# Feed-forward units of 128-token blocks: one slice of the inner width each, or two

## The chip, the core and the metric

The kernel runs on one core of a Trainium2 chip. Its time is the device time of one execution in microseconds (us), the median of three runs. The engines are named as in the profile: PE is TensorE (matmuls; PEld its weight loads), DVE is VectorE, ACT is ScalarE, POOL is GpSimd and SP is SyncE, which issues most DMAs.

## What is computed

Three stages follow each other: attention that keeps the 32 best scores of each row (4 batches, 8 heads, 576 tokens, head size 64), a feed-forward layer on the 2304 tokens that come out, and a layer of 8 experts of which each token uses one or none.

```
scores = (q @ k.T) / sqrt(64); keep those >= the 32nd largest of the row; softmax; x = attn @ v
h = x @ w_in                    # 2304 x 512 by 512 x 2048
r = max(h, 0); g = r * r
x = g @ w_out                   # 2304 x 2048 by 2048 x 512
out = x; tokens with x @ w_skip > 0: out = x + gate * (max(x @ w1[e], 0) @ w2[e]), e = argmax(x @ w_gate)
```

The change is in the second stage.

## The kernel before, in words

**Attention.** The main loop makes 76 ticks `j`. A tick takes one pair of score tiles (128 queries by 576 keys each). For the next pair `qk` (line 311) puts the scores into PSUM on PE and `evac_s` (line 330) copies them out on ACT (line 332); both have high priority. On DVE a tick is `tree` (line 355, work on line 360) for the next pair, `top32` (line 366: MAX8 and MATCH_REPLACE8 four times) and `mask` (line 404). ACT does the exponential (line 401) and its 16-bit high part (line 430), POOL multiplies by the mask (line 415) and takes the low part (line 435). Three ticks later `av` (line 445) multiplies by v on PE, `xout` scales the rows, and `x_split` (line 487) splits a finished block of 128 tokens into two 16-bit parts and sends it through a transposing DMA to `xt`.

**Groups and units.** Tokens come in groups (`group`, line 95): 14 groups of 128 tokens (the halved blocks, and the two `c` groups of the batches' first tokens) and 2 groups of 256. `add_units` (line 523) cuts a group that is ready, two ticks after its x was sent, into 16 units, one for each slice of 128 columns of the inner width 2048. A unit goes through four steps:

- `mm1` (line 529) on PE: 12 matmuls (line 535) of the group's tokens against one slice of `w_in`, as high x high, low x high and high x low parts, into a PSUM tile `ph` (two buffers of 256 columns).
- `act1` (line 540) on ACT: the copy through the rectifier `r` (line 543), the square `g` in 32 bits (line 545) and the square `gh` in 16 bits (line 547). `r` and `g` have two buffers, `gh` four; all are 256 columns wide, and a unit of 128 tokens uses half.
- `g_low` (line 553) on POOL: the remainder `g - gh` (line 556).
- `mm2` (line 561) on PE: for each 128 tokens three matmuls of 512 columns (line 568), accumulated in `px` over the 16 slices. Behind the last slice `finish` copies the rows out and stores them; transposes and logits for the experts' gate follow.

**The order.** `step_units(n)` (line 615) adds n to a credit and, while it holds one, takes the next unit: `mm1` of it, `act1` of the one before, `mm2` of the oldest whose remainder was asked for; it then takes off the unit's columns divided by 128. A tick calls it twice with 2.2 (`HALVES` is 4.4, line 40) and calls `g_low` once, later. Behind the attention the loop on line 913 drains what is left with `step_units(1, 1)`, `g_low` and the logits, one unit a turn. When the tokens of a stretch of groups are through, `route` (line 776) and `first_ids` (line 824) work out their experts on DVE, with small matmuls on PE (lines 797, 798, 801 and 831) and tiles `oh`, `cum` and `hit`; their entries are scattered to a table by POOL (line 837), one a turn and only while fewer than `DRAIN` = 12 units (line 52) are left. Ahead of this loop 16 chunks of the experts' weights are split on ACT, DVE and POOL (`next_chunk`, line 889). After it the last route, the scatters left over and the first gather (line 961) start the experts.

The queue of each engine is fixed when the program is built: the instructions are taken in the order of the source, high priority first, against a modelled timeline (line 1407), and an engine then runs its queue in that order.

Of the kernel before, what the change touches and what calls it, by code (L numbers as in the profile page):

```python
# [9 lines left out]
F32 = mybir.dt.float32  # L10
# [12 lines left out]
NTOK, DM, DFF = B * S, 512, 2048  # L23
# [25 lines left out]
ON_POOL = (4, 6)  # L49
BG = (3, 3, 2)  # L50
PRE = 16
DRAIN = 12
X_EXP, M_EXP = 12, 7
XBUFS = [4, 2, 2]
BUFS = {"qm": 2, "ql": 2, "qc": 2, "k": 4, "v": 8}
# [44 lines left out]
def attention_two_moes(ctx, tc, qm, qc, kd, vd, w_in, w_out, w_g, w1, w2, cst, out):  # L100
    nc = tc.nc
    const = ctx.enter_context(tc.tile_pool(name="const", bufs=1))
    dram = ctx.enter_context(tc.tile_pool(name="dram", bufs=1, space=DRAM))
    psum = ctx.enter_context(tc.tile_pool(name="psum", bufs=1, space=PSUM))
# [24 lines left out]
    wil = wpool.tile([128, 4, DFF], F16, name="wil")  # L129
    wol = wpool.tile([128, 16, DM], F16, name="wol")  # L130
    wih = wpool.tile([128, 4, DFF], F16, name="wih")
    woh = wpool.tile([128, 16, DM], F16, name="woh")
# [388 lines left out]
    units = []  # L521

    def add_units():
        while ready and tick[0] >= max(ready[0][1] + X_LAG, UNIT_START):
            gr = ready.pop(0)[0]
            for f in range(16):
                units.append(dict(gr=gr, f=f, n=128 * len(gr[1])))

    def mm1(u):
        x = xt[u["gr"]]  # L530
        ph = psum.tile([128, 256], F32, name="ph", bufs=2)[:, :u["n"]]
        n = 0
        for wt, c0 in ((wih, 0), (wih, 4), (wil, 0)):
            for d in range(4):
                nc.tensor.matmul(ph, lhsT=wt[:, d, u["f"] * 128:(u["f"] + 1) * 128], rhs=x[:, :, c0 + d, :],  # L535
                                 start=(n == 0), stop=(n == 11))
                n += 1
        u["ph"] = ph

    def act1(u):  # L540
# [18 lines left out]
    x2p = {}  # L559

    def mm2(u):
        f, gh, gr = u["f"], u["gh"], u["gr"]
        if f == 0:
            x2p[gr] = [psum.tile([128, DM], F32, name="px", bufs=2) for _ in gr[1]]
        for t, px in enumerate(x2p[gr]):
            n = 0
            for part, w in ((0, woh), (0, wol), (1, woh)):
                nc.tensor.matmul(px, lhsT=gh[:, part, t * 128:(t + 1) * 128], rhs=w[:, f, :],  # L568
                                 start=(f == 0 and n == 0), stop=(f == 15 and n == 2))
                n += 1  # L570
        if f == 15:
            finish(gr)

# [2 lines left out]
    def finish(gr):  # L576
        kk = gr[0]
        for px, t in zip(x2p[gr], gr[1]):
            n = column(kk, t)
            x2 = mpool.tile([128, DM], F32, name="x2", tag="x2", bufs=2)  # L580
            nc.scalar.activation(x2, px, AF.Copy, scale=2.0 ** -OUT_EXP)
            if kk == "c":
                for a in range(2):
                    r0 = (2 * t + a) * S
                    stores.append(nc.sync.dma_start(out[r0:r0 + 64, :], x2[64 * a:64 * a + 64, :]))
            else:
                r0 = kk[0] * S + 64 + 256 * kk[1] + 128 * t
                stores.append(nc.sync.dma_start(out[r0:r0 + 128, :], x2))
            logit_jobs.append((x2, n))
# [25 lines left out]
    def step_units(n, depth=0):  # L615
        add_units()
        credit[0] += n
        while credit[0] > 0.99:
            u = units.pop(0) if units else None
            if u:  # L620
                mm1(u)
            if started:
                act1(started.pop(0))
            if u:
                started.append(u)
            if len(lowered) > (depth if u else 0):
                mm2(lowered.pop(0))
            credit[0] -= u["n"] / 128 if u else 2
            if not u:
                credit[0] = min(credit[0], 0)  # L630
# [26 lines left out]
    start = by_j.pop(-1)  # L657
# [186 lines left out]
    wt = {}  # L844
# [63 lines left out]

    tick[0] = NJ + 9
    add_units()  # L910
    edge, marks = 0, [NT - 4, NT - 2] + [NT - 1] * (LAST in HALVED)
    pending = []
    while units or started or squared or lowered:
# [5 lines left out]
        while marks and min(left, default=NT) >= marks[0]:  # L919
# [3 lines left out]
            edge = marks.pop(0)  # L923
        if pending and len(units) < DRAIN:
            with tc.issue_after(g_last[0]):
# [485 lines left out]
```

## Time and profile before

| | us |
|---|---|
| median of 3 runs | 1027.3 |
| the three runs | 1027.3, 1023.33, 1030.25 |
| the profiled execution | 1023.65 |
| its span, first to last instruction | 1021.8 |

The profile is of one execution. Start times count from the beginning of the span; busy times are sums over one engine. A row of the timeline gives the start, the duration, the engine, the line, the operation, what it writes and reads, and in brackets how long its engine stood idle before it and what ended that. Operations of one kind in a row are merged (x2), and their durations overlap at the ends.

### The profile page before, as it was taken

Reading aid. Unit: us, or ns where it says so; the run is one execution under the profiler, and the core shown is the slowest. Engines: PE = TensorE matmul, PEld = TensorE weight load, DVE = VectorE, ACT = ScalarE, POOL = GpSimd, SP = SyncE. Lnnn points to the kernel's source line nnn. Section 1 sums busy time; section 2 is a strip of 40 time slices with the busy share of each in tenths; the row PEclk is TensorE's granted clock in tenths of the full one; section 3 lists DMA queues with packets and bytes.
Section 4 is the critical chain, followed back from the end, with each engine's and each line's share of the span. In section 5 each row is a group of like instructions: output and inputs, shape, how many; then the busy total and the mean of one; then the engine's idle time right before and its main releaser. Section 6 shows DMA issues by size and latency. Waiting matters only on the chain. (4 is left out here: it accounts for less than half of the span.)

```text
span 1021.8 us, 25759 instructions
## 1 busy us (share of the span) xinstructions
PE 779.8 (76%) x9036; PEld 592.5 (58%) x9036; DVE 845.7 (83%) x2279; ACT 759.8 (74%) x2117; POOL 767.4 (75%) x783
## 2 busy tenths in 40 slices
PE   0123337989879979989969999999997958688852
PEld 0122226767667757667657777767775746565631
DVE  4999999999999999999989999999908634535631
ACT  7777676899988998888779989999866642544620
POOL 4576777899879898888879988899955875744850
PEclk9999999999999999999979999999998978898876
DMA  9675554668675475565475676565537508653500
GB/s 286 174 189 152 141 126 78 103 137 156 118 161 111 94 150 94 108 130 119 100 137 121 138 138 130 116 117 90 96 64 269 208 27 326 214 177 113 177 15 10
DMA packets 257023, 138.16 MB, mean 135 GB/s; under 512 B 215348, under 2 KB 238260, under 8 KB 256848
## 3 DMA queue, kind: packets, MB, share of 16 engines
q1 hardware_dynamic: 253568, 132.16, 55.7%
q0 software_dynamic: 3280, 3.80, 1.2%
q8 instruction: 94, 1.54, 0.6%
q14 instruction: 81, 0.66, 0.2%
HBM read 76.92 MB, written 7.37 MB: 82 GB/s over the span
## 5 line engine op out<-in xcount | busy, mean ns | idle before, releaser
L379 DVE MAX8 m<-tr 128x8 f32<-128x288 f32 (+1 forms) x576 | 275.8, 517 | 0.0
L435 POOL TENSOR_TENSOR phl<-e,phl 128x576 f16<-128x576 f32 x144 | 190.6, 1328 | 33.2 <-ACT phl L430 29.0
L415 POOL TENSOR_TENSOR e<-e,mk 128x576 f32<-128x576 f32 x144 | 196.0, 1371 | 21.9 <-DVE mk L406 21.9
L568 PE MATMUL px<-woh,gh 128*128 128x512 f16 x576 | 189.3, 382 | 15.9 <-POOL gh L556 10.8
L382 DVE MATCH_REPLACE8 tr<-m,tr 128x288 f32<-128x288 f32 x432 | 186.8, 437 | 0.0
L535 PEld LDWEIGHTS <-wih 128*128 128x128 f16 x2048 | 143.2, 101 | 55.4 <-issue 23.6
L535 PE MATMUL ph<-xb,wih 128*128 128x128 f16 (+1 forms) x1792 | 156.6, 231 | 21.0 <-DMA xb<-xhl 9.5
L458 PE MATMUL misc<-vh,pt 128*128 128x64 f16 (+1 forms) x2400 | 119.3, 198 | 63.7 <-ACT xn L476 33.7
L556 POOL TENSOR_TENSOR gh<-g,gh 128x128 f16<-128x128 f32 (+1 forms) x256 | 130.2, 515 | 41.1 <-ACT gh L547 27.4
L458 PEld LDWEIGHTS <-pt 128*128 128x128 f16 (+1 forms) x2400 | 100.8, 100 | 85.3 <-issue 53.2
L568 PEld LDWEIGHTS <-gh 128*128 128x128 f16 x864 | 77.5, 100 | 86.0 <-POOL gh L556 21.1
L360 DVE SCALAR_TENSOR_TENSOR tr<-pS,s 128x576 f32<-128x576 f32 x144 | 102.1, 750 | 14.8 <-ACT s L332 10.8
L401 ACT ACTIVATE e<-s,nm 128x576 f32<-128x576 f32 x144 | 111.0, 772 | 1.4 <-POOL phl L435 0.7
L568 PE MATMUL px<-wol,gh 128*128 128x512 f16 x288 | 109.7, 382 | 0.0
L430 ACT ACTIVATE phl<-e 128x577 f16<-128x577 f32 x144 | 98.0, 681 | 2.8 <-POOL e L415 2.8
L543 ACT ACTIVATE r<-ph 128x128 f32<-128x128 f32 (+1 forms) x256 | 70.3, 287 | 37.9 <-PE ph L535 36.8
L535 PE MATMUL ph<-xb,wil 128*128 128x128 f16 (+1 forms) x896 | 97.4, 230 | 0.0
L326 PE MATMUL pS<-kh,ql 128*128 128x192 f16 x576 | 67.2, 273 | 38.9 <-DMA kh<-lp 26.1
L406 DVE TENSOR_SCALAR mk<-s,m 128x576 f16<-128x576 f32 x144 | 93.3, 688 | 0.0
L545 ACT ACTIVATE g<-r 128x128 f32<-128x128 f32 (+1 forms) x256 | 82.7, 324 | 7.1 <-POOL gh L556 3.4
L332 ACT ACTIVATE s<-pS 128x1152 f32<-128x1152 f32 x72 | 80.3, 1116 | 3.7 <-PE pS L326 3.4
L547 ACT ACTIVATE gh<-r 128x128 f16<-128x128 f32 (+1 forms) x256 | 80.7, 320 | 1.3 <-PE px L568 1.0
(229 smaller groups left out, 1585.6 us busy)
## 6 DMA issues: line engine op xcount, KB each, us to landing
wraw<-in_w SPq DMA_DIRECT2D x64, 512.0 KB, 5.4
wol<-in_w_in SPq DMA_DIRECT2D x16, 512.0 KB, 4.9
raw<-in_qm SPq DMA_DIRECT2D x48, 128.0 KB, 2.8
w<-in_w_out SPq DMA_DIRECT2D x10, 512.0 KB, 3.7
raw<-in_vd SPq DMA_DIRECT2D x32, 160.0 KB, 2.8
raw<-in_kd SPq DMA_DIRECT2D x16, 288.0 KB, 3.5
out<-x SPq DMA_DIRECT2D x16, 256.0 KB, 2.6
wol<-in_w_out SPq DMA_DIRECT2D x6, 512.0 KB, 3.7
```

The source lines that it names most:

```text
L360: last = nc.vector.scalar_tensor_tensor(out=R2[:, :, n * 288:n * 288 + 288].rearrange("p k (c x) -> p k c x", c=3), in0=near, scalar=2.0 * ...
L379: return both(lambda k: nc.vector.max(m[k][:, 8 * r:8 * r + 8], x[k][:, :n]))
L382: both(lambda k: nc.vector.match_replace(out=dst[k][:, :n], in_to_replace=m[k][:, 8 * r:8 * r + 8], in_values=src[k][:, :n], imm_value=NEG))
L401: nc.scalar.activation(e[:, :S], st[i]["s"], AF.Exp, scale=0.125, bias=st[i]["nm"])
L406: nc.vector.tensor_scalar(out=t, in0=st[i]["s"], scalar1=st[i]["m"][:, 31:32], scalar2=None, op0=ALU.is_ge)
L415: nc.gpsimd.tensor_mul(e[:, :S], e[:, :S], st[i]["mk"])
L430: nc.scalar.activation(h[:, 0, :S + 1], st[i]["e"], AF.Copy, accum_out=st[i]["l"][:, 0:1])
L435: nc.gpsimd.tensor_sub(h[:, 1, :S], st[i]["e"][:, :S], h[:, 0, :S])
L458: nc.tensor.matmul(ps[:, a, :], lhsT=pt[:rows, 5 * low + c, :], rhs=vh[:rows, c, part * D:(part + 1) * D], start=(n == 0), stop=(n == len( ...
L535: nc.tensor.matmul(ph, lhsT=wt[:, d, u["f"] * 128:(u["f"] + 1) * 128], rhs=x[:, :, c0 + d, :], start=(n == 0), stop=(n == 11))
L556: g_last[0] = nc.gpsimd.tensor_sub(u["gh"][:, 1], u["g"], u["gh"][:, 0]).ins
L568: nc.tensor.matmul(px, lhsT=gh[:, part, t * 128:(t + 1) * 128], rhs=w[:, f, :], start=(f == 0 and n == 0), stop=(f == 15 and n == 2))
```

## The change

A unit of a 128-token group now takes two neighbouring slices, so that every unit is 256 columns wide. `add_units` makes 8 such units of a group (a 256-token group keeps its 16). `mm1` runs the 12 matmuls for the one slice into the first half of `ph`, then the 12 for the other into the second half; `act1` and `g_low`, which are not edited, work on all 256 columns; `mm2` runs three matmuls for each slice. A unit costs two credits. `DRAIN` counts units and goes from 12 to 6.

```
-DRAIN = 12
+DRAIN = 6
...
     def add_units():
         while ready and tick[0] >= max(ready[0][1] + X_LAG, UNIT_START):
             gr = ready.pop(0)[0]
-            for f in range(16):
-                units.append(dict(gr=gr, f=f, n=128 * len(gr[1])))
+            step = 2 // len(gr[1])
+            for f in range(0, 16, step):
+                units.append(dict(gr=gr, fs=range(f, f + step), n=256))
 
     def mm1(u):
         x = xt[u["gr"]]
-        ph = psum.tile([128, 256], F32, name="ph", bufs=2)[:, :u["n"]]
-        n = 0
-        for wt, c0 in ((wih, 0), (wih, 4), (wil, 0)):
-            for d in range(4):
-                nc.tensor.matmul(ph, lhsT=wt[:, d, u["f"] * 128:(u["f"] + 1) * 128], rhs=x[:, :, c0 + d, :],
-                                 start=(n == 0), stop=(n == 11))
-                n += 1
+        ph = psum.tile([128, 256], F32, name="ph", bufs=2)
+        for i, f in enumerate(u["fs"]):
+            w = 256 // len(u["fs"])
+            n = 0
+            for wt, c0 in ((wih, 0), (wih, 4), (wil, 0)):
+                for d in range(4):
+                    nc.tensor.matmul(ph[:, i * w:i * w + w], lhsT=wt[:, d, f * 128:(f + 1) * 128], rhs=x[:, :, c0 + d, :],
+                                     start=(n == 0), stop=(n == 11))
+                    n += 1
         u["ph"] = ph
...
     def mm2(u):
-        f, gh, gr = u["f"], u["gh"], u["gr"]
-        if f == 0:
-            x2p[gr] = [psum.tile([128, DM], F32, name="px", bufs=2) for _ in gr[1]]
-        for t, px in enumerate(x2p[gr]):
-            n = 0
-            for part, w in ((0, woh), (0, wol), (1, woh)):
-                nc.tensor.matmul(px, lhsT=gh[:, part, t * 128:(t + 1) * 128], rhs=w[:, f, :],
-                                 start=(f == 0 and n == 0), stop=(f == 15 and n == 2))
-                n += 1
+        gh, gr = u["gh"], u["gr"]
+        for i, f in enumerate(u["fs"]):
+            if f == 0:
+                x2p[gr] = [psum.tile([128, DM], F32, name="px", bufs=2) for _ in gr[1]]
+            for t, px in enumerate(x2p[gr]):
+                n = 0
+                for part, w in ((0, woh), (0, wol), (1, woh)):
+                    nc.tensor.matmul(px, lhsT=gh[:, part, (t + i) * 128:(t + i + 1) * 128], rhs=w[:, f, :],
+                                     start=(f == 0 and n == 0), stop=(f == 15 and n == 2))
+                    n += 1
         if f == 15:
             finish(gr)
```

## Rows read from the trace of the kernel before

**Rows 1.** Busy time of each engine in two stretches (count), granted clock, DMA.

```profile
core 0: us, PE busy (x) PEld busy (x) DVE busy (x) ACT busy (x) POOL busy (x), PEclk, DMA share, GB/s
190.00:740.00 550.00, 503.93 (x6172) 385.15 (x6171) 540.85 (x1557) 489.61 (x1502) 480.67 (x529) 0.98 0.64 122
740.00:830.00 90.00, 78.46 (x835) 58.07 (x832) 43.80 (x142) 55.97 (x180) 59.63 (x79) 0.96 0.50 155
```

**Rows 2.** DVE's waits from 100 to 742 us: total us, times, longest.

```profile
DVE tr L360 <- ACT s L332: 5.1, 3, 3.4
```

**Rows 3.** Groups by shape: count, busy us, mean ns of one, idle before, releasers.

```profile
L543 ACT ACTIVATE r<-ph 128x128 f32<-128x128 f32 x224 | 58.4, 273 | 32.7 <-PE ph L535 31.7
L543 ACT ACTIVATE r<-ph 128x256 f32<-128x256 f32 x32 | 12.0, 379 | 5.2 <-PE ph L535 5.1
...
L545 ACT ACTIVATE g<-r 128x128 f32<-128x128 f32 x224 | 69.3, 310 | 6.9 <-POOL gh L556 3.4 <-ACT nm L387 0.3
L545 ACT ACTIVATE g<-r 128x256 f32<-128x256 f32 x32 | 13.5, 421 | 0.2
...
L547 ACT ACTIVATE gh<-r 128x128 f16<-128x128 f32 x224 | 67.3, 306 | 1.3 <-PE px L568 1.0
L547 ACT ACTIVATE gh<-r 128x256 f16<-128x256 f32 x32 | 13.4, 419 | 0.0
...
L556 POOL TENSOR_TENSOR gh<-g,gh 128x128 f16<-128x128 f32 x224 | 108.1, 489 | 38.8 <-ACT gh L547 25.2 <-ACT g L545 5.5 <-DMA wraw<-in_w 2.2
L556 POOL TENSOR_TENSOR gh<-g,gh 128x256 f16<-128x256 f32 x32 | 22.1, 696 | 2.3 <-ACT gh L547 2.3
```

**Rows 4.** ACT's timeline near 401 us.

```profile
400.96 0.53 ACT L547 ACTIVATE gh<-r 128x128 f16<-128x128 f32 x2
```

**Rows 5.** POOL's subtractions of line 556 from 740 to 830 us, busy us (count).

```profile
740.00:830.00 90.00, 26.72 (x48) 0.96 0.50 155
```

**Rows 6.** Timeline of DVE and PE where DVE waited longest.

```profile
493.83 1.42 DVE L360 SCALAR_TENSOR_TENSOR tr<-pS,s 128x576 f32<-128x576 f32 x2 [1.26 <-ACT s L332]
...
525.21 1.89 PE L535 MATMUL ph<-xb,wih 128*128 128x256 f16 x8 [2.82 <-DMA xb<-xhl]
...
532.60 1.42 DVE L360 SCALAR_TENSOR_TENSOR tr<-pS,s 128x576 f32<-128x576 f32 x2 [3.36 <-ACT s L332]
```

**Rows 7.** Timeline of ACT and DVE in a tick without a wait.

```profile
402.66 1.11 ACT L332 ACTIVATE s<-pS 128x1152 f32<-128x1152 f32 x1
...
408.34 1.42 DVE L360 SCALAR_TENSOR_TENSOR tr<-pS,s 128x576 f32<-128x576 f32 x2
```

**Rows 8.** PE's timeline in the drain.

```profile
761.20 0.61 PE L535 MATMUL ph<-xb,wih 128*128 128x128 f16 x8
...
762.51 0.59 PE L568 MATMUL px<-woh,gh 128*128 128x512 f16 x2
...
786.48 1.01 PE L535 MATMUL ph<-xb,wih 128*128 128x128 f16 x8
```

**Rows 9.** The mask of line 406, all of it: ns min/median/max, first and last start.

```profile
L406 DVE TENSOR_SCALAR mk<-s,m x144: 500/592/1536, 34.2 to 740.0; 128x576 f16<-128x576 f32 x144
```

**Rows 10.** PE's waits from 740 to 830 us: total us, times, longest.

```profile
PE pS L831 <- DVE hit L830: 3.9, 4, 2.1
PE misc L797 <- DVE oh L790: 2.7, 1, 2.7
...
PE ph L535 <- ACT r L543: 0.8, 1, 0.8
```

**Rows 11.** POOL's timeline at the end of the drain.

```profile
826.83 0.99 POOL L837 DMA_INDIRECT table<-ent,sloti  x1 [0.17 <-issue]
827.85 0.44 POOL L556 TENSOR_TENSOR gh<-g,gh 128x128 f16<-128x128 f32 x1
828.46 0.99 POOL L837 DMA_INDIRECT table<-ent,sloti  x1 [0.17 <-issue]
829.76 0.97 POOL L837 DMA_INDIRECT table<-ent,sloti  x1 [0.30 <-issue]
```

**Rows 12.** Busy times by stretch, columns as in rows 1.

```profile
780.00:790.00 10.00, 5.18 (x38) 4.27 (x37) 8.53 (x30) 5.99 (x15) 6.30 (x6) 0.76 0.38 135
```

## The prediction, made before the change was run

> **What bounds the kernel now.** I read the busy times of the two stretches that hold feed-forward units first [rows 1], because each has its own limit. From 190 to 740 us the attention runs beside the feed-forward units: DVE is busy for 540.85 of 550 us, PE for 503.93, ACT for 489.61, POOL for 480.67. DVE sets the pace there, and its waits say so too: between 100 and 742 us the longest was 5.1 us in all, of the tree on line 360 for the scores that line 332 copies [rows 2]. From 740 to 830 us the remaining units drain: PE is busy for 78.46 of 90 us, DVE for 43.80, ACT for 55.97, POOL for 59.63, so PE is nearest to the bound. Then the experts run on code that the diff does not touch; they start when the last unit's rows have been stored, routed and gathered, and so they shift by whatever the drain shifts. The question is therefore what the change does to DVE before 740 us, and to PE and the tail of the drain after it.
>
> **What the change does to the work.** There are 14 groups of 128 tokens and 2 of 256, so 224 units of the narrow form and 32 of the wide one [rows 3]. Afterwards the 224 become 112 of the wide form. PE's work does not change: each slice still has its 12 matmuls of 128 columns and its 3 of 512, with the same weights, in another grouping.
>
> ACT: per pair of slices, one copy and two squares of 256 columns replace two copies and four squares of 128. By mean durations [rows 3] that is 2 x 273 - 379 = 167 ns, 2 x 310 - 421 = 199 ns and 2 x 306 - 419 = 193 ns, together 0.56 us. But the operations overlap: two narrow squares of some 0.32 us each took 0.53 us back to back [rows 4], so 0.11 us of each lies under its neighbour; for the wide ones I take the same. Three operations fewer lose 0.33 us of that overlap, and 0.23 us per pair is left: 26 us for 112 pairs. Of the subtractions 48 came after 740 us [rows 5], all of the last groups' narrow form, so some 176 narrow slices, 88 pairs, lie in the attention: 20 us of ACT's time there. POOL: 2 x 489 - 696 = 0.28 us per pair [rows 3], 32 us in all, 25 us of it in the attention.
>
> **What of that reaches the end, in the attention.** ACT and POOL wait there for others as it is; a shorter operation makes them wait longer. What can be won is only DVE's own 5.1 us [rows 2]. Of these, 1.26 and 3.36 us [rows 6] are two single stalls. In the second, PE had stood for 2.82 us in front of matmuls whose transposed x had not landed; the scores were queued behind them. The change moves neither that load nor the two ticks by which the unit lags behind it. So I take 1 us of the 5.1 us; the ends are 0 and 5.1. The other way about, the scores are normally early: the copy that DVE needs at 408.34 us was issued at 402.66 us and took 1.11 us, 4.6 us to spare [rows 7]. A wide unit holds PE for one more slice, 12 matmuls, about 0.7 us (in the drain a slice's 12 and 3 together took 1.31 us, from 761.20 to 762.51 us [rows 8], and 8 of the 12 are 0.61 of them): that is hidden by the 4.6 us, and costs DVE nothing unless PE is late for another reason already.
>
> DVE's mask (line 406) takes between 0.50 and 1.54 us, 0.59 in the middle [rows 9], so something holds it up; which operation, these rows don't say, and POOL's are the nearest neighbours. Longer subtractions could hold a mask longer, fewer could meet it less often. If one mask in each of the 40 ticks with narrow units (176 slices at 4.4 a tick) met a subtraction longer by 0.21 us (696 - 489 ns [rows 3]) it would cost 8 us; if one in each tick missed one, it would save about as much. Half the number at one and a half times the length comes out about even, so I take 0 and keep +8 and -8 for the range.
>
> **The credits.** A unit now costs two credits, the tick still gives 4.4. Counted through the 76 ticks by the code, 17 slices are queued at the end before, 16 after, beside the last group's 16. So the drain begins with the same work: no gain, no loss (the odd slice, 1.3 us, is only started earlier; I count 0.2 us for it).
>
> **The drain.** PE's waits here are 3.9 us for the `hit` tiles, 2.7 us for `oh`, and 0.8 us for ACT's copy of `ph` [rows 10]. The first two are the routing's matmuls, queued on PE between units, waiting for DVE; the change doesn't touch them. With 48 subtractions left [rows 5] ACT and POOL give back 24 x 0.23 = 5.5 us and 24 x 0.28 = 6.7 us, nearly all beside PE. I take the 0.8 us of PE's wait on ACT's copy and 1 us for the routing's waits, since DVE, ACT and POOL are less crowded; ends 0 and 4.
>
> The tail is different. At its end POOL alternates without a gap: subtraction to scatter 0.61 us, scatter to subtraction 1.02 us, scatter to scatter 1.30 us [rows 11]. Per two slices that was 2 x 1.63 = 3.26 us, over PE's 2 x 1.31, so POOL sets the end. After: one wide subtraction (0.61 + 0.21) and two scatters (1.30 + 1.02) is 3.14 us. Six pairs win 0.7 us. Against it: scatters begin when fewer than 6 units are left instead of 12, which is 10 slices instead of 11, up to 1.3 us later, part of it absorbed by gaps that POOL still has when the scatters begin; the last subtraction is longer by 0.21 us; and behind it up to four matmuls wait instead of one, 0.2 to 0.65 us. Together +0.5 us, ends -0.7 and +1.5.
>
> **Sum.** -1 (attention) -0.8 -1 (drain) +0.5 (tail) = -2.3 us, -2.5 with the odd slice. The profiled execution took 1023.65 us, of which its span is 1021.8; it would take 1021.2. It lies 3.65 us under the median of the runs, 1027.3, so for that median I forecast 1024.8 us. A measurement of this kernel can tell about 1%, 10 us, from no change; this is not that.
>
> **A rule of the Trainium skill.** ACT was busy for 89% of the attention, DVE for 98% [rows 1]. The skill's page Trace Analysis, section Optimizing Scalar/DVE Operations, says that grouping into larger operations helps throughput where the engine is saturated, and that where ACT is not saturated but causes bubbles elsewhere, breaking instructions up lets work finish sooner. By the first half the 20 us would come off; by the second the change goes the wrong way. The two rivals below are worked out from the rows alone.
>
> **Rivals.** *ACT is the real bound.* If the DVE-paced tick hid an ACT that is never free when needed, the 20 us of the attention would come off, and 3 in the drain: 1027.3 - 23 = 1004 us. Against it: DVE waits for ACT's copy only 5.1 us in 642 [rows 2]. Chance 0.03. By the skill's rule of grouping this is what a saturated ACT would give.
>
> *The drain's stalls go.* The queue of PE is ordered when the program is built, and another grain of units gives another order. If the routing's matmuls fall later, the 3.9 + 2.7 us go, and with them the slow clock behind them: at 786 us, behind that wait, eight matmuls took 1.01 us instead of 0.61 [rows 8], and the granted clock was 0.76 between 780 and 790 us [rows 12], which is 1.2 GHz instead of 2.4 for 4.8 us, or 2.4 us lost. 1024.8 - 9.0 = 1015.8 us. For it: nothing else in the drain is as large; against it: DVE's routing chain is the same. Chance 0.12.
>
> *Coarser units stall DVE.* Both large stalls of DVE [rows 6] lie in the 15 ticks or so (64 slices' worth of credits at 4.4) in which the wide units already run; in the 40 ticks of narrow ones it lost only 5.1 - 4.6 = 0.5 us. If the width is the cause (a block of 24 matmuls in front of the scores, behind a load that is late), the rate of 4.6 / 15 = 0.31 us a tick comes to 40 x 0.31 = 12.4 us: 1027.3 + 12.4 - 1.3 (the drain's part of the sum) = 1038.4 us. It decides once PE is late by over 4.6 us in a tick. Against it: those two groups also wait for two transposes instead of one, and a block is only 0.7 us longer. By the skill's second half, breaking up, this is the expected harm. Chance 0.12.
>
> **How the numbers follow.** 0.73 for the forecast, whose own range is 1018 to 1033 with the mask's ends. With 0.12 + 0.03 on the fast side, 0.12 on the slow side, the range that holds 8 in 10 is 1015 to 1036 us. Faster by over 1%: 0.15; within 1%: 0.72; slower by over 1%: 0.13 (0.01 for an order that no row suggests).
>
> **What would show it.** Right: 144 copies of some 379 ns and 144 subtractions of some 696 ns where there were 256 each; ACT's busy time between 190 and 740 us lower by some 49 us (0.56 x 88) with DVE's unchanged to a few us; the last subtraction ending within 4 us of 828.29 us, where it ends now [rows 11]; POOL's pattern one subtraction to two scatters. Wrong: a tree that waits for the scores in many ticks (the slow rival), an attention that ends over 10 us earlier (the first rival), or a drain without waits on `hit` and `oh` (the second).

## The result: 10 us less, from a drain that begins with less work

| | before | after |
|---|---|---|
| median, us (7 runs each) | 1026.22 | 1015.75 |
| lowest to highest | 1023.23 to 1030.25 | 1013.66 to 1018.55 |
| the profiled execution | 1023.65 | 1014.78 |
| its span | 1021.8 | 1013.0 |

The ratio is 0.9904, with a 95% interval of 0.9878 to 0.9929. The forecast was 1024.8 us in a range of 1015 to 1036: the time lies just inside the range, four times as far from the old one as forecast (10.5 us against 2.5).

Start with the busy times in the two stretches of [rows 1], now of the kernel after (columns as there):

```profile
190.00:740.00 550.00, 506.69 (x6187) 395.10 (x6186) 538.29 (x1548) 469.93 (x1241) 463.88 (x443) 0.96 0.63 121
740.00:830.00 90.00, 75.56 (x762) 55.18 (x760) 52.07 (x180) 52.88 (x115) 58.23 (x59) 0.89 0.51 159
```

ACT and POOL have 19.7 and 16.8 us less to do between 190 and 740 us, DVE 2.6 us. In the second row PE shows fewer matmuls, 762 for 835. Which are gone? The same stretch for the first matmuls of the units alone, line 535 before and 538 after (PE busy, count; weight loads; clock):

```profile
740.00:830.00 90.00, 38.05 (x540) 34.64 (x540) 0.96 0.50 155
```

```profile
740.00:830.00 90.00, 30.30 (x432) 28.09 (x432) 0.89 0.51 159
```

540 matmuls are 45 slices, 432 are 36: nine slices fewer were left at 740 us. So I split each span at two rows: the last `tree` of DVE, where the attention's pace ends, and the last second matmul of the units (`px`). The group rows of the kernel after (ns min/median/max, first and last start):

```profile
L360 DVE SCALAR_TENSOR_TENSOR tr<-pS,s x144: 735/747/759, 21.3 to 734.4; 128x576 f32<-128x576 f32 x144
...
L572 PE MATMUL px<-woh,gh x576: 376/379/634, 172.9 to 820.3; 128*128 128x512 f16 x192
```

The last pair of trees starts at 733.7 us, the second of the two at 734.4. From the pair to 820.3 are 86.6 us; before, from 730.2 to 828.3, it was 98.1. The four parts of the 8.8 us between the spans are (rounded): 1.3 us gained up to the tree near 151 us, before any unit has run, 4.9 us lost in the attention (from that tree to the last: 578.1, then 583.0), 11.5 us gained in the drain, 0.8 us gained behind it.

**The attention.** Summed over DVE's timeline from the tree near 151 us to the last, the 4.9 us are 3.0 us more standing idle (6.2, then 9.2, in gaps of over 0.15 us), 3.0 us more on the low part of v (line 245: 18.8, then 21.8) and 1.4 us less on masks (80.0, then 78.6). Its waits from 100 to 742 us (as in [rows 2]), and the longest and the shortest of the three for the copies of the scores:

```profile
DVE tr L360 <- ACT s L332: 7.3, 3, 3.1
...
DVE tr L360 <- ACT r L546: 0.5, 1, 0.5
```

```profile
531.49 1.42 DVE L360 SCALAR_TENSOR_TENSOR tr<-pS,s 128x576 f32<-128x576 f32 x2 [3.05 <-ACT s L332]
...
615.43 1.42 DVE L360 SCALAR_TENSOR_TENSOR tr<-pS,s 128x576 f32<-128x576 f32 x2 [1.76 <-ACT s L332]
```

The first is the old stall of 3.36 us [rows 6]. The second is new, and so is the third, of 2.46 us at 644.5 us. Ahead of the stall at 615 us the twelve matmuls of a tick's scores stand in PE's queue in two halves, and 4.7 us of other work, 4.1 of them second matmuls, lie between.

```profile
606.34 0.66 PE L326 MATMUL pS<-kh,ql 128*128 128x192 f16 x6
...
611.55 0.66 PE L326 MATMUL pS<-kh,ql 128*128 128x192 f16 x6
```

The scores were complete at 612.2 us, and ACT came to copy them only at 614.27. It is ACT's queue that held them up, and not the split on PE: from 600 us to the copy ACT shows no gap of over 0.15 us, so that it would have come to a complete tick of scores no sooner. The last operation ahead of the copy, and the copy:

```profile
613.89 0.36 ACT L221 ACTIVATE raw<-raw 128x192 f32<-128x192 f32 x1
614.27 1.13 ACT L332 ACTIVATE s<-pS 128x1152 f32<-128x1152 f32 x1
```

**The groups by shape** (as in [rows 3]) are as the diff says, 144 of each, with nearly the forecast durations:

```profile
L559 POOL TENSOR_TENSOR gh<-g,gh 128x256 f16<-128x256 f32 x144 | 103.0, 718 | 43.2 <-ACT gh L550 41.3 <-PE misc L458 0.9 <-ACT lg_all L612 0.5
L548 ACT ACTIVATE g<-r 128x256 f32<-128x256 f32 x144 | 60.0, 417 | 2.3
L550 ACT ACTIVATE gh<-r 128x256 f16<-128x256 f32 x144 | 59.2, 412 | 4.5 <-PE px L572 4.4
L546 ACT ACTIVATE r<-ph 128x256 f32<-128x256 f32 x144 | 54.3, 378 | 25.2 <-PE ph L538 24.6
```

**The drain's waits** on the routing (as in [rows 10]) did not go; the queue has another order:

```profile
PE pS L835 <- DVE hit L834: 4.6, 2, 3.9
PE misc L802 <- DVE cum L796: 4.5, 1, 4.5
PE misc L801 <- DVE oh L794: 1.5, 1, 1.5
```

This window now reaches past the last second matmul at 820.3 us. The wait for `oh` and 0.7 us of those for `hit` come behind it:

```profile
825.20 0.60 PE L801 MATMUL misc<-oh,cs 128*128 128x8 f32 x2 [1.46 <-DVE oh L794]
827.31 0.59 PE L835 MATMUL pS<-tokm,hit 128*128 128x1 f32 x2 [0.66 <-DVE hit L834]
```

Within the drain the waits on `hit`, `cum` and `oh` were 7.5 us before (3.9, 0.9 and 2.7), and are 8.4 after and 6.7 in a second profile of the change (e12 below). Two other waits of the kernel before are gone or nearly so: the 0.8 us for ACT's copy [rows 10], and the one for POOL's remainders (none after, 0.8 us in e12):

```profile
PE px L568 <- POOL gh L556: 2.4, 5, 0.8
```

In all, PE stands idle for less of the drain, not for more: 10.8 us before, 8.8 after, 8.0 in e12. From the last pair of trees to the last second matmul, before and then after (length, PE's busy time and count, granted clock, DMA):

```profile
730.20:828.30 98.10, 87.30 (x969) 0.97 0.51 152
733.70:820.30 86.60, 77.76 (x853) 0.92 0.56 173
```

Behind the long waits matmuls are slower, as in [rows 8]. Eight matmuls of line 538 soon behind the wait for `cum`, where the granted clock was 0.50, 1.2 GHz (776 to 780 us), and the same eight later, where it was 0.99 (780 to 784 us):

```profile
776.42 0.77 PE L802 MATMUL misc<-cum,ones 128*128 128x112 f32 x2 [4.47 <-DVE cum L796]
...
778.05 1.06 PE L538 MATMUL ph<-xb,wih 128*128 128x128 f16 x8
...
781.65 0.61 PE L538 MATMUL ph<-xb,wih 128*128 128x128 f16 x8
```

**The tail** of POOL (as in [rows 11]) is one subtraction to two scatters, 3.14 us from this subtraction to the next at 818.87 us, as forecast:

```profile
815.73 0.69 POOL L559 TENSOR_TENSOR gh<-g,gh 128x256 f16<-128x256 f32 x1
816.58 0.99 POOL L841 DMA_INDIRECT table<-ent,sloti  x1 [0.17 <-issue]
817.88 0.97 POOL L841 DMA_INDIRECT table<-ent,sloti  x1 [0.30 <-issue]
```

### The profile page after: what moved, and what is told of

The parts are those of the page before. It is cut to its first block, busy times and chain, and to the rows that moved or that the text cites. A ratio compares the mean times of both kernels' runs of the same rounds, so it can differ in the third digit from the quotient of the medians.

```text
span 1013.0 us, 25026 instructions
## 1 busy us (share of the span) xinstructions
PE 779.2 (77%) x9036; PEld 600.8 (59%) x9036; DVE 847.9 (84%) x2279; ACT 732.1 (72%) x1781; POOL 745.0 (74%) x671
## 5 line engine op out<-in xcount | busy, mean ns | idle before, releaser
L435 POOL TENSOR_TENSOR phl<-e,phl 128x576 f16<-128x576 f32 x144 | 188.5, 1316 | 34.3 <-ACT phl L430 32.9
L572 PE MATMUL px<-woh,gh 128*128 128x512 f16 x576 | 185.6, 384 | 1.1 <-POOL gh L559 1.1
L458 PE MATMUL misc<-vh,pt 128*128 128x64 f16 (+1 forms) x2400 | 122.3, 201 | 69.8 <-ACT xn L476 39.4
L538 PE MATMUL ph<-xb,wih 128*128 128x128 f16 (+1 forms) x1792 | 163.4, 232 | 9.1 <-DMA xb<-xhl 7.4
L458 PEld LDWEIGHTS <-pt 128*128 128x128 f16 (+1 forms) x2400 | 103.1, 102 | 88.2 <-issue 57.9
L559 POOL TENSOR_TENSOR gh<-g,gh 128x256 f16<-128x256 f32 x144 | 103.0, 718 | 43.2 <-ACT gh L550 41.3
L572 PEld LDWEIGHTS <-gh 128*128 128x128 f16 x864 | 81.8, 99 | 82.5 <-issue 3.0
L326 PEld LDWEIGHTS <-ql 128*128 128x128 f16 x576 | 56.0, 110 | 44.1 <-ACT wih L303 17.3
L538 PEld LDWEIGHTS <-wil 128*128 128x128 f16 x1024 | 73.8, 100 | 2.7
L546 ACT ACTIVATE r<-ph 128x256 f32<-128x256 f32 x144 | 54.3, 378 | 25.2 <-PE ph L538 24.6
```

The source lines that it names most:

```text
L326: nc.tensor.matmul(ps[:, c], lhsT=q[:, part], rhs=kh[:, c * 192:(c + 1) * 192], start=(n == 0), stop=(n == 2 * len(jobs) - 1))
L435: nc.gpsimd.tensor_sub(h[:, 1, :S], st[i]["e"][:, :S], h[:, 0, :S])
L458: nc.tensor.matmul(ps[:, a, :], lhsT=pt[:rows, 5 * low + c, :], rhs=vh[:rows, c, part * D:(part + 1) * D], start=(n == 0), stop=(n == len( ...
L538: nc.tensor.matmul(ph[:, i * w:i * w + w], lhsT=wt[:, d, f * 128:(f + 1) * 128], rhs=x[:, :, c0 + d, :], start=(n == 0), stop=(n == 11))
L559: g_last[0] = nc.gpsimd.tensor_sub(u["gh"][:, 1], u["g"], u["gh"][:, 0]).ins
L572: nc.tensor.matmul(px, lhsT=gh[:, part, (t + i) * 128:(t + i + 1) * 128], rhs=w[:, f, :], start=(f == 0 and n == 0), stop=(f == 15 and n = ...
```

## How much work stands behind the last scores

Of the 11.5 us that the drain is shorter, 2.0 are idle time of PE and 9.5 are time that it works less. So the drain begins with less work. The time of the last scores hardly differs (PE's timeline, before and then after):

```profile
725.04 1.15 PE L326 MATMUL pS<-kh,ql 128*128 128x192 f16 x12
```

```profile
726.87 1.15 PE L326 MATMUL pS<-kh,ql 128*128 128x192 f16 x12
```

What differs is what stands behind them. PE's queue is fixed when the program is built, so it can be counted without the chip: before, 54.0 slices of first matmuls and 55.3 of second stand behind the last scores, after the change 44.8 and 52.0. A slice's first twelve matmuls took 0.67 us (781.65 to 782.32 us) and its second three 0.645, so 9.2 and 3.3 slices fewer are 8.3 of the 11.5 us.

The credits in the source are the same to one slice. But the queue is not the source's order: instructions are placed against a modelled timeline, and a first matmul can be placed ahead of its turn as far as there is a free `ph`, then a free `r` and `g`, then a free `gh`. These are 256 columns wide, and a 128-token unit used half of each. With two slices in a unit the same buffers hold twice the slices. That was the first theory, **room**. Its rival was **fewer operations**: ACT and POOL, with 20 and 17 us less to do, let PE run on.

Here are all the kernels. The first columns are counted from the queue, the next three from each kernel's profile; the last is the median of the runs. "Behind" is the sum of slices of first and of second matmuls behind the last scores; "drain" runs from the last tree to the last second matmul; "attention" from the tree near 151 us to the last.

| kernel | behind | drain, us | attention, us | DVE idle, us | median, us |
|---|---|---|---|---|---|
| before | 54.0 + 55.3 = 109.3 | 98.1 | 578.1 | 6.2 | 1025.3 to 1026.2 |
| after | 44.8 + 52.0 = 96.8 | 86.6 | 583.0 | 9.2 | 1015.75 |
| after, again (e12) | the same | 86.5 | 583.3 | 8.8 | 1015.94 |
| e1, small operations | 46.0 + 53.3 = 99.3 | 88.7 | 574.2 | 1.7 | 1008.12 |
| e1 again (e11) | the same | 89.4 | 578.5 | 3.4 | 1010.93 |
| e2, one `r`, one `g` | 50.0 + 56.0 = 106.0 | 92.8 | 582.9 | 5.7 | 1022.99 |
| e3, one `ph` | 54.0 + 57.7 = 111.7 | 100.5 | 583.5 | 2.4 | 1027.84 |
| e4, narrow, four `r`, four `g` | 49.8 + 54.3 = 104.1 | 95.2 | 575.9 | 2.7 | 1023.3 |
| e5, small ACT, wide POOL | 46.9 + 52.0 = 98.9 | 88.7 | 588.8 | 9.5 | 1019.45 |
| e6, wide ACT, small POOL | 45.5 + 53.0 = 98.5 | 87.3 | 581.0 | 5.5 | 1014.54 |
| e7, DRAIN 12 | 44.8 + 52.0 = 96.8 | 87.0 | 581.6 | 6.4 | 1020.03 |
| e8, narrow, 5.0 credits | 53.2 + 56.0 = 109.2 | 97.1 | 579.9 | 5.1 | 1026.08 |
| e9, wide before tick 66 | 46.4 + 50.3 = 96.7 | 89.2 | 584.3 | 7.3 | 1026.75 |
| e10, wide from tick 66 | 50.5 + 58.0 = 108.5 | 97.2 | 580.3 | 5.6 | 1025.14 |

## The experiments

The kernels ran in three sets (e1 to e4, e5 to e8, e9 to e12) on three chips, each beside runs of the kernel before, whose median was 1025.75 us (25 runs), 1026.14 (24) and 1025.32 (23).

**e1: two slices to a unit, but the old small operations.** The matmuls and the buffers are the change's; ACT and POOL work on each half of 128 columns by itself, as before.

```
+        H = [slice(128 * i, 128 * i + 128) for i in range(len(u["fs"]))] if len(u["fs"]) == 2 else [slice(0, 256)]
+        for h in H:
+            nc.scalar.activation(r[:, h], u["ph"][:, h], AF.Relu, scale=2.0 ** -R_EXP)
...
+            two = len(u["fs"]) == 2
+            for h in ([slice(0, 128), slice(128, 256)] if two else [slice(0, 256)]):
+                g_last[0] = nc.gpsimd.tensor_sub(u["gh"][:, 1, h], u["g"][:, h], u["gh"][:, 0, h]).ins
```

> The units keep their two slices, but ACT and POOL work on each half by itself: one copy, two squares and one remainder of 128 columns for each slice, as before the change. Theory of room (a unit of two slices fills the buffers ph, r, g and gh, which a unit of 128 tokens left half empty, so that PE's queue runs further ahead and less is left when the attention ends): in PE's queue 46.0 slices' first matmuls stand behind the last scores, against 44.8 after the change and 54.0 before, so nearly the whole gain stays: 1015 to 1018 us. Theory of fewer operations (the gain comes from the 26 us of ACT and 32 us of POOL that the wide operations save): all of it goes, 1024 to 1028 us.

1008.12 us (4 runs, 1006.5 to 1009.54), ratio 0.982 (0.9773 to 0.9867). All the operations are back, and the gain is not smaller but larger, 7 us under the expected range. Fewer operations as the source of the gain is refuted.

**e2: the change with one `r` and one `g`.**

```
-        r = mpool.tile([128, 256], F32, name="r", bufs=2)[:, :w]
+        r = mpool.tile([128, 256], F32, name="r", bufs=1)[:, :w]
...
-        g = mpool.tile([128, 256], F32, name="g", bufs=2)[:, :w]
+        g = mpool.tile([128, 256], F32, name="g", bufs=1)[:, :w]
```

> The changed kernel with one buffer each for r and g instead of two, so that they hold two slices, as before the change; the operations stay wide. Theory of room: 50.0 slices stand behind the last scores in PE's queue and 36 behind the last product with v (44.8 and 29.9 after the change, 54.0 and 37.0 before); 6 more slices of first matmuls at 0.67 us and 1.3 of second at 0.65 give +5 us, 1019 to 1023 us. Theory of fewer operations: no change from the changed kernel, 1014 to 1018 us.

1022.99 us (10 runs), ratio 0.9982 (0.9955 to 1.0009): with as many slices of `r` and `g` as before, the gain is gone, though the operations are the wide ones. About half of it goes in the drain, 92.8 us between 98.1 and 86.6; the attention is as long as the change's.

**e3: the change with one `ph` for the units** (transposes and gate keep one of their own, in the other bank).

```
-        ph = psum.tile([128, 256], F32, name="ph", bufs=2)
+        ph = psum.tile([128, 512], F32, name="phu", bufs=1)[:, :256]
```

> The changed kernel with one PSUM buffer for the units' first product instead of two, so that it holds two slices, as before the change (the other bank serves the logits); the operations stay wide. Theory of room: 54.0 slices stand behind the last scores in PE's queue and 40 behind the last product with v, so all of the gain goes, 1023 to 1030 us; PE also has to wait for each copy. Theory of fewer operations: 1014 to 1019 us.

1027.84 us (10 runs), ratio 1.0011 (0.9987 to 1.0035). The queue behind the last scores is longer than before the change, and so is the drain.

**e4: the kernel before with four `r` and four `g`.**

```
-        r = mpool.tile([128, 256], F32, name="r", bufs=2)[:, :w]
+        r = mpool.tile([128, 256], F32, name="r", bufs=4)[:, :w]
...
-        g = mpool.tile([128, 256], F32, name="g", bufs=2)[:, :w]
+        g = mpool.tile([128, 256], F32, name="g", bufs=4)[:, :w]
```

> The kernel before, units of one slice, with four buffers for r and g instead of two; gh (four) and ph (two) as before. Theory of room: 49.8 slices stand behind the last scores and 35.1 behind the last product with v (54.0 and 37.0 before), so 2 to 4 us come off without any change of the units, 1022 to 1025 us. Theory of fewer operations: 1026 us, no change.

1023.3 us (10 runs, 1017.56 to 1025.54), ratio 0.9965 (0.9938 to 0.9991): room alone, with the narrow units, gives a part of the gain and of the shorter queue.

**e5 and e6: which small operations?** e1 was 7.6 us under the change. e5 has small operations on ACT only, e6 on POOL only.

> Units of two slices; ACT's copy and squares again on each half of 128 columns, POOL's subtraction on all 256. In PE's queue, as fixed when the program is built, 31.2 slices of first and 37.7 of second matmuls stand behind the last product with v (after the change 29.9 and 38.0, with all operations small 29.1 and 38.0): so the drain is as long as the change's to 1 us by every theory, and the difference of 7.6 us between the change and the kernel with all operations small lies in the attention. Theory A (ACT's wide operations hold up the copies of the scores or the exponentials, and so DVE): the attention from the tree of tick 9 to the last is back at 564 us, and the time is 1008 us +-3. Theory P (POOL's wide subtractions hold up DVE's masks and splits of v through what the two engines share): the attention stays at 573 us and the time at 1016 us +-3. Theory O (the order of the queues alone, no width): neither, and this run and the next do not share the loss out between them; both near one end, or one of them outside.

> Units of two slices; ACT's copy and squares on all 256 columns, as in the change, POOL's subtraction on each half of 128. Behind the last product with v 29.7 and 38.0 slices stand in PE's queue. Theory A: 1016 us +-3, attention 573 us. Theory P: 1008 us +-3, attention 564 us. Theory O: not the mirror image of the run before.

(These expectations and e8's count the attention from a tree 10 us later than the table does: 573 us there are 583.0 here.)

1019.45 us (8 runs), ratio 0.9936 (0.991 to 0.9962), and 1014.54 us (5 runs), ratio 0.9895 (0.9856 to 0.9933). Neither comes near e1. Theory A wanted 1008 of e5, theory P wanted it of e6: both fall as stated. O, the order of the queues, is left of the three; that the gain needs small operations on both engines at once is not excluded either. Only one trace of P remains: the stall near 615 us is there where POOL's wide subtraction goes with the change's buffers (1.76 us after the change, 1.77 again, 2.55 in e5, 1.76 in e7, 1.79 in e9), and not in e1, e6 and e11. It doesn't settle the time: e6 is as slow as the change without it.

**e7: the edit of DRAIN alone undone.**

```
-DRAIN = 6
+DRAIN = 12
```

> The change with DRAIN left at 12 units, so that scatters may begin when 22 slices are left, not 10. Queue of PE as in the change (29.9 and 38.0 slices behind the last product with v). If the edit of DRAIN is worth nothing: 1015.8 us +-3 and the same pattern of one subtraction to two scatters at the tail, or fewer scatters in the tail and up to 3 us less. Rival: earlier scatters take POOL from the subtractions while PE still waits for little, and the drain gets longer by up to 10 of 1.0 us.

1020.03 us (10 runs, 1012.01 to 1027.16), ratio 0.9945 (0.9915 to 0.9974). The interval meets that of the change (0.9878 to 0.9929) at its end. So 12 is not better than 6 and may be some 4 us worse; the profiled execution took 1012.01 us, so its trace cannot show where. That stays open.

**e8: a shorter queue by more credit?** The kernel before, with 5.0 credits a tick.

```
-HALVES = 4.4
+HALVES = 5.0
```

> The kernel before with units of one slice and its buffers, but 5.0 credits a tick instead of 4.4. In PE's queue 30.0 slices of first and 36.0 of second matmuls stand behind the last product with v, as after the change (29.9 and 38.0; before 37.0 and 42.3), without any unit of two slices. Theory of the queue (what is left of the units when the attention ends sets the time, whatever the unit's width): the drain gets shorter by 7.0 x 0.67 + 6.3 x 0.645 = 8.8 us, the attention, with no wide operation, stays at 566 to 568 us, and the time is 1015 to 1019 us. Rival (the wider unit itself shortens the drain, by fewer operations on ACT and POOL): the drain is the old one or PE waits more in it, and the time is 1023 us or more.

1026.08 us (10 runs), ratio 0.9999 (0.9976 to 1.0021). A miss, and a useful one: I had counted what stands behind the last product with v. The group row of that product in e8:

```profile
L458 PE MATMUL misc<-vh,pt x2400: 189/193/261, 47.6 to 764.0; 128*128 128x64 f16 x148, 64*128 64x64 f16 x37
```

In the kernel before it ends with 753.2. The 7 slices had moved ahead of the last product, and the product had moved 11 us back: nothing had left the drain. The first matmuls from 740 to 830 us in e8 are the old 540:

```profile
740.00:830.00 90.00, 37.77 (x540) 34.21 (x540) 0.98 0.51 158
```

The count that holds is the one behind the last scores, because DVE sets when those come. By it e8 has 109.2, as before.

**e9 and e10: width in the drain, or ahead of it?** e9 has units of two slices for the groups cut before tick 66, e10 for the later ones, whose units fill the drain.

```
-            step = 2 // len(gr[1])
+            step = 2 // len(gr[1]) if tick[0] < 66 else 1
```

(e10 has `>= 66`.)

> Units of two slices only for groups that are cut before tick 66; the groups cut later, which fill the drain, have units of one slice as before. DRAIN stays at 6 units. In PE's queue, as fixed when the program is built, 46.4 slices of first and 50.3 of second matmuls stand behind the last scores, together 96.7 (the change: 44.8 and 52.0, together 96.8; before: 54.0 and 55.3, together 109.3). Theory of the queue (the slices behind the last scores set the length of the drain, whatever the width of the units in it; the nine kernels so far lie on one line, from 96.8 and 86.6 us to 111.7 and 100.5 us between the last tree and the last second matmul): 86 to 89 us, and with an attention of 574 to 583 us 1008 to 1017 us. Theory of the narrow drain (fewer operations on ACT and POOL in the drain make it shorter): 95 us or more, and 1021 us or more.

> The mirror image: units of one slice for groups cut before tick 66, of two slices for the later ones, which fill the drain. Behind the last scores 50.5 and 58.0 slices stand in PE's queue, together 108.5. Theory of the queue: 96 to 99 us between the last tree and the last second matmul, and 1020 to 1027 us. Theory of the narrow drain: the drain of the change, 87 us, and 1008 to 1016 us.

1026.75 us (12 runs), ratio 1.0012 (0.9989 to 1.0034), and 1025.14 us (12 runs), ratio 0.999 (0.9967 to 1.0012). The drains came out as the queue says, 0.2 us over the upper end in e9: the last trees and second matmuls of e9,

```profile
L360 DVE SCALAR_TENSOR_TENSOR tr<-pS,s x144: 741/749/777, 21.9 to 737.8; 128x576 f32<-128x576 f32 x144
...
L572 PE MATMUL px<-woh,gh x576: 376/379/634, 174.5 to 826.3; 128*128 128x512 f16 x192
```

and of e10:

```profile
L360 DVE SCALAR_TENSOR_TENSOR tr<-pS,s x144: 741/749/768, 21.3 to 731.0; 128x576 f32<-128x576 f32 x144
...
L572 PE MATMUL px<-woh,gh x576: 376/379/634, 171.1 to 827.5; 128*128 128x512 f16 x192
```

89.2 us with narrow units in the drain, 97.2 with wide ones: width there shortens little by itself. e9, with as much in its queue as the change (96.7 and 96.8), takes 2.7 us longer than its 86.5 to 86.6. The shorter drain comes from the wide units *ahead* of tick 66, which leave less for the end. The time of e9 I missed by 10 us, mainly for two reasons outside the drain. The attention took 584.3 us, 6.2 more than before and 1.3 over the 583 allowed for. And DRAIN was still 6 units, now of one slice, so that the scatters began with 6 slices left and outlasted the units. POOL at e9's end, the last subtraction, the first and the last of the scatters between it and the gather, and the gather that starts the experts:

```profile
825.77 0.45 POOL L559 TENSOR_TENSOR gh<-g,gh 128x128 f16<-128x128 f32 x1
826.39 0.99 POOL L841 DMA_INDIRECT table<-ent,sloti  x1 [0.17 <-issue]
...
839.20 1.67 POOL L841 DMA_INDIRECT table<-ent,sloti  x1 [0.30 <-issue]
841.17 1.05 POOL L965 DMA_INDIRECT xg<-out,idx  x1 [0.30 <-issue]
```

and the same place in the kernel after:

```profile
818.87 0.69 POOL L559 TENSOR_TENSOR gh<-g,gh 128x256 f16<-128x256 f32 x1
819.72 0.99 POOL L841 DMA_INDIRECT table<-ent,sloti  x1 [0.17 <-issue]
...
824.85 0.97 POOL L841 DMA_INDIRECT table<-ent,sloti  x1 [0.30 <-DVE gate L797]
828.37 1.04 POOL L965 DMA_INDIRECT xg<-out,idx  x1 [2.55 <-DVE sloti L819]
```

Eleven scatters stand between the last subtraction and the gather instead of five, and the gather comes 14.9 us behind the last second matmul instead of 8.1.

**e11 and e12: the small operations and the change, side by side.**

> Units of two slices with ACT's and POOL's operations on each half of 128 columns, once more, beside the change on one chip. If the small operations are worth something by themselves: at least 4 us under the change in the same call, 1006 to 1010 us, with an attention near 574 us. If the 7.6 us were the difference of two chips or of single executions: within 3 us of the change.

> The change, once more, unedited, beside the run before. 1013 to 1019 us; its attention in the profile shows how far two executions of one kernel lie apart (583.0 us the first time).

1010.93 us (6 runs, 1005.71 to 1013.04), ratio 0.9851 (0.982 to 0.9883), against 1015.94 us (6 runs, 1012.81 to 1017.53), ratio 0.9894 (0.9867 to 0.9921). The difference is 5.0 us on one chip; the two intervals still overlap a little, and the 7.6 us between e1 and the change in the earlier runs point the same way. Where it lies, two pairs of profiles tell only in part (e11 against e12, e1 against the change): the attention is shorter by 4.8 and 8.8 us, the drain longer by 2.9 and 2.1, and the stage behind the first gather shorter by 4.2 and 2.4. The attention came out at 578.5 us where 574 was expected, 4.3 longer than in e1, the same kernel. What is the same in both is that DVE stands idle for less: 1.7 and 3.4 us against 9.2 and 8.8. Its waits for the copies of the scores, in e11 and then in e5 and e6:

```profile
DVE tr L360 <- ACT s L332: 1.1, 2, 0.6
DVE tr L360 <- ACT s L332: 6.7, 4, 2.7
DVE tr L360 <- ACT s L332: 2.9, 2, 2.4
```

The stage behind the first gather, from its start to the end of the span, runs the same code in every kernel (but for PSUM tiles in e3), and took 181.3 us (e11) to 188.8 us (e10), 184.3 before and 184.6 after the change. Differences of a few us between the other kernels' times may come from there.

And the small operations are all paid for: ACT is busy for 490.06 of 550 us, 22.7 more than in e12 (467.34) and as long as before the change (busy times of e11):

```profile
190.00:740.00 550.00, 505.97 (x6223) 394.78 (x6220) 544.17 (x1556) 490.06 (x1518) 480.11 (x533) 0.96 0.65 122
740.00:830.00 90.00, 74.39 (x730) 55.70 (x728) 47.90 (x173) 53.70 (x160) 59.24 (x77) 0.90 0.51 157
```

That costs the end nothing here. The version with two slices to a unit and small operations beats both kernels: the one before by 14 to 18 us, the one after by 5 to 8 us.

## Why the prediction was right, and where it was not

It was right in sign and range, and its largest term was missing.

**The step that failed is "So the drain begins with the same work: no gain, no loss".** It was counted from the credits in the source. The queue of PE runs ahead of the source as far as its buffers allow, and the change doubled the slices that they hold: 9.2 and 3.3 slices fewer stand behind the last scores, and the drain is 11.5 us shorter. e2 and e3 take the room back and with it the gain (e2 in the drain only half of it); e1 shows that room without fewer operations is enough; e4 that it is worth something to narrow units too. Over the fourteen profiles of the table a straight line gives 0.86 us of drain for each slice of either kind, with none over 2.3 us off it. The matmuls alone are worth 0.66 us, the mean of 0.67 and 0.645; between the two kernels 2.0 us are idle time of PE, and what makes up the rest wasn't tried. The front of the document had the two facts from which the term follows: the buffers are 256 columns wide and half used, and the queue is ordered by a modelled timeline. I worked out what a unit costs and not what its buffers let through.

**Attention, forecast -1 us, ends 0 and -5.1; measured +4.9.** Outside the ends. I let only DVE's old stalls shrink; a new order made new ones. Two executions agree (583.0 and 583.3 us), against 578.1 in the one profile of the kernel before; since e1 and e11, one kernel, lie 4.3 us apart, the size is not sure.

**ACT and POOL, forecast 20 us less busy for ACT in the attention; measured 19.7.** The overlap at the ends of back-to-back operations [rows 4] was rightly taken off. What would show it, "some 49 us", was not: it multiplied the mean durations without that overlap and contradicts the 20. POOL's 25 were 16.8.

**Masks, forecast 0, ends -8 and +8; measured -1.4 and +0.9 us in two executions.** Right.

**Drain's waits, forecast -1.8 us; PE's idle time there fell by 2.0 and 2.8 us in two executions.** The size is right, the waits are in part others. The routing's, forecast 1 us less, went from 7.5 to 8.4 and 6.7 us; the 0.8 us for ACT's copy are gone as forecast; and the sum leaves out the 2.4 us for POOL's remainders, of which none and 0.8 us were left. That fewer operations did this is not shown: e1 and e11, with small ones, have PE idle for 8.4 and 9.0 us.

**Tail, forecast +0.5 us.** The cycle is the forecast 3.14 us, and one subtraction stands to two scatters. The drain was so much shorter for another reason that the half microsecond itself can't be read. For that reason a sign of being right failed too: the last subtraction was to end within 4 us of 828.29 us, and ended at 819.56.

**The rivals.** *ACT is the real bound* is refuted: the 20 us were saved and didn't come off, and e11 has them back and is faster. *The drain's stalls go* named the right time (1015.8 us, measured 1015.75) for a wrong reason: the stalls stayed. (Its sum also counts 1 us of the routing's waits twice.) That is an accident, and worth remembering: a time that fits is no evidence for its mechanism. *Coarser units stall DVE* was half true: the attention did lengthen by DVE's waits, by 3.0 us of idle time and not by 12.4. Against its reason, a block of 24 matmuls in front of the scores, speak e1 and e11, whose units have the same 24 and where DVE stands idle for only 1.7 and 3.4 us.

The Trainium skill's page Perfetto Trace Analysis, section Optimizing Scalar/DVE Operations, says that grouping can help a saturated engine, and that breaking up may help where ACT is not saturated but holds others up. The traces bear out neither half by itself. ACT, busy for 89% of the attention, was not the bound, and the grouping shortened nothing there. With all operations small DVE waits 1.1 us for the copies of the scores (e11) where the change has 7.3; but e5, small on ACT alone, has 6.7, and e6, wide on ACT, 2.9.

**What stays open.** Why the small operations make the kernel faster: e5 and e6 don't share the gain out between ACT and POOL, which speaks for the order that the model gives the queues, and no kernel changed that order alone. Why the stage behind the first gather differs by some us between kernels. And whether DRAIN at 12 costs 4 us.

## What to carry to other kernels

Where an engine's queue is ordered at build time, count in that queue what stands behind the last instruction that the critical engine needs; credits and loops in the source don't tell, and nor does a count behind an instruction that can itself move (e8). A buffer that a unit half fills is look-ahead given away: make the unit fill it, and choose the size of the operations on the side engines separately. And a saving on an engine that was busy for 89% of a stage was worth nothing here, since DVE hardly waited for it.

## What was not expected of the hardware

Small operations on ACT and POOL cost busy time but not pace: two copies of 278 ns for one of 378, two squares of 318 for one of 417, two subtractions of 456 for one of 718, and the attention was no longer with them, 4.8 us shorter in e11 than in e12. Their rows in e11:

```profile
L565 POOL TENSOR_TENSOR gh<-g,gh 128x128 f16<-128x128 f32 x224 | 98.1, 456 | 23.2 <-ACT gh L554 22.4 <-POOL gh L565 0.6
L551 ACT ACTIVATE g<-r 128x128 f32<-128x128 f32 x224 | 70.0, 318 | 0.1
...
L548 ACT ACTIVATE r<-ph 128x128 f32<-128x128 f32 x224 | 49.5, 278 | 22.6 <-PE ph L538 20.1 <-PE px L578 2.0
```

And single executions of one kernel on one chip lie up to 15 us apart (e7, 1012.01 to 1027.16) with no change in what they run; the change itself kept within 5 us in both of its sets of runs.
